# A gated mix of linear attention and a bilinear GLU on one core: thirteen places for h and w_down in the first pair, longer leads for the weights' factors, joint products two steps sooner

## The chip, the cores and the metric

The kernel runs on one NeuronCore of a Trainium2 chip. Its metric is the time of one execution in microseconds (us): the median of three runs before the change is 619.75 us (619.34 to 624.1). All tensors are float32. The matmuls take float32r operands, and every float32 operand is split into a high part (rounded to float32r by a copy) and a low part (the rest), so a product of two operands is three matmuls: high by high, high by low, low by high.

## The reference

The input x has 2048 rows (tokens) of 512. Cut to what matters:

```python
g = sigmoid((x * gate_w).sum(-1, keepdims=True))
# a: linear attention, 32 heads of 16
q, k, v = split_heads(x @ wqkv)
phi = lambda t: where(t > 0, t + 1, exp(t)) + 1e-6
kv  = einsum("bhsd,bhse->bhde", phi(k), v);  z = phi(k).sum over tokens
o   = (phi(q) @ kv) / (phi(q) . z + 1e-6)
a   = o @ wo
# b: bilinear GLU, width F = 1792
h = (x @ w_gate) * (x @ w_up)
b = h @ w_down
return g * a + (1 - g) * b
```

## The kernel before

A first phase computes phi(k) and its products with x for all tokens, and prepares sums of blocks of x. It isn't touched by the change.

The second phase goes over the tokens in two **pairs** of blocks of 512 tokens, and in each pair over 16 **units** (32 in all, numbered n from 0): 14 are of kind "f", one for each 128 columns of F, and two are of kind "q", which make q for half of the heads. A unit multiplies a 2 by 2 arrangement of weight blocks with a 2 by 2 arrangement of blocks of x in seven products of sums of blocks (Strassen's scheme; function `unit`). Each product is six matmuls of 128x512. They go into four PSUM banks Y, X, R and S, each with one buffer, in the order Y X Y R X R S. Between them, by program order, ACT copies Y to m2 (`m` in the profile) and cross, DVE makes R = X - m2, t, S = t - X, and at the end the two products cross that are the two blocks of h. ACT and DVE split these into high and low (tiles `slot`).

All instructions keep the order in which the program writes them, on each engine: ACT, DVE, PE, and the DMA queues of SP and POOL run in order, and an instruction that waits holds all that stand behind it on its engine. So the place of a piece of work in the unit matters. A unit has named **places**, in this order: high, low, e, m, c, d, t, s, r, end. `later(n, place, fn)` puts work at a place, `do` runs it. In a unit ACT also makes the next unit's weights: `w_high` (`wch` in the profile) and the scaled copies for the unit after it (`wr<-wr`), to which POOL adds blocks by DMA (`wr<-in_wgu_add`). SP loads `wr` (`w_load`).

**Down jobs.** Two f units make a group: their two h tiles (high, low) and two w_down tiles are six places. A group gives eight jobs (`down_jobs`), each six matmuls `pdn<-slot,slot` for 128 tokens, scaled and summed into `acc` by DVE. A unit takes jobs from the list at four places, after e, c, t and s, and `shares` tells how many at each: the default is one each, and a table gives other numbers for single units. Jobs not there aren't taken.

**Places for h and w_down.** `slot()` hands out nine tiles of 128x1024 float32r (`SLOTS`) in a circle: three for each f unit, given back when the group's last job has been issued. The w_down tile of a group's first unit is split at "e", that of its second at "r" (`down_weights`), and the split is followed by the next w_down load on SP.

**Mixed units.** In the second pair the four units f4 to f7 (n = 22 to 25) don't make places: their h stays float32 in four tiles `hraw` (scaled by `keep`, two tiles of the pool tag `cb`), since it goes into joint products with the attention's output.

**Output products.** The attention's output is multiplied by a matrix made of kv and wo. This again is a scheme of seven products (`OPROD`), run by `products`. For each product a weight factor is loaded by SP (`w_raw`, `wraw`), has a second block added by POOL (`w_sum`), and is split by ACT and DVE (`w_split`, `owh`, `owl`); the left factor is loaded and added (`load`, `add`, `oraw`) or made from `hraw` (`h_sum`), split at `ready` (`oh`, `ol`), and used by two output jobs of 12 matmuls `po` of 128x256, which `o_down` issues one share later. In the second pair each product has two halves that add up in one bank ("joint"): one of kind "h" with h's blocks and w_down's, and one of kind "o". So there are 28 lines, one a **step**; the second pair has five steps a unit (e, c, t, s, end), the first four (e, c, t, end). Step 0 of the second pair is step 132 counted from unit 0: unit 26, place "t". A weight factor's split stands one step before its first use, its sum two steps before the split, its load four. The factors lie in the tag `cb` (three buffers), the left factors in `z` and `ph` in turn (four each), which before that hold the attention's intermediate tiles (`ex`, `zq`, `zt`, `rb`; `phq`).

After the last unit the last group's eight jobs run, and SP stores the output.

Of the kernel before, what the change touches and what calls it, by code (L numbers as in the profile page):

```python
# [7 lines left out]
F32 = mybir.dt.float32  # L8
F32R = mybir.dt.float32r
# [5 lines left out]
P = 128  # L15
# [8 lines left out]
CH = 512  # L24
# [5 lines left out]
LEAD = 4  # L30
HB = 8
SLOTS = 9
HALF = D // 2


# [27 lines left out]
def gated_mix(ctx: ExitStack, tc, xt, xp, x, wqkv, wq, wq_add, wo, wgu, wgu_add, wdn, gate_w, out):  # L63
# [349 lines left out]
    def unit(n, quad, mixed):  # L413
# [72 lines left out]
        if quad:  # L486
            quad(1, 1, bank["R"])
        elif mixed:
            tt(mixed[:, 1], bank["R"], cross[:, 1], ALU.mult)
        else:  # L490
            hh, hl = hidden()
            tt(cross[:, 1], bank["R"], cross[:, 1], ALU.mult)
            act(hh[:, 1], cross[:, 1])
        do(n, "r")
        product(7, "S")
        if quad:
            quad(0, 0, bank["S"])
        elif mixed:
            tt(mixed[:, 0], bank["S"], cross[:, 0], ALU.mult)
        else:  # L500
            tt(cross[:, 0], bank["S"], cross[:, 0], ALU.mult)

            def high(c):
                act(hh[:, c], cross[:, c])

            def low(c):
                tt(hl[:, c], cross[:, c], hh[:, c].bitcast(F32), ALU.subtract)

            if n + 1 < len(order):

                low(1)
                later(n + 1, "high", lambda: high(0))
                later(n + 1, "low", lambda: low(0))
            else:

                high(0)
                for c in 1, 0:
                    later(n, f"low{c}", lambda c=c: low(c))
            return hh, hl
# [11 lines left out]
    def hidden():  # L531
        return [slot() for _ in "hl"]

    def o_tiles():
        return [p2.tile([P, D], F32R, tag=f"o{v}", name=f"o{v}", bufs=2) for v in "hl"]
# [105 lines left out]
    def down_jobs(pair, group):  # L641
# [3 lines left out]
        def job(i):  # L645
# [12 lines left out]
            for o in range(0, D, step):  # L658
                cols = slice(o, o + step)
                banks.reverse()  # L660
                pd = psum.tile([P, D], F32, tag=banks[0], name="pdn", bufs=2)[:, 0:step]
                for j, ((hh, hl), w2) in enumerate(group):
                    mm3(pd, (hh[:, c, sl], hl[:, c, sl]), [w2[:, v, cols] for v in range(2)], j == 0, j == 1)
                a = acc[pair, i // 2][:, i % 2, cols]
                if first:
                    act(a, pd, scale=s)
                else:
                    stt(a, pd, s, a, ALU.mult, ALU.add)
                if ends:
                    to = nc.gpsimd if pair == 0 else nc.sync  # L670
                    tc.keep_in_program_order(to.dma_start(out[t * P:(t + 1) * P, cols], a))
            todo[0] -= 1
            if not todo[0]:
                for hid, w2 in group:
                    free.extend((*hid, w2))

        return [lambda i=i: job((i + TPP // 2) % TPP) for i in range(TPP)]

# [83 lines left out]
    rows_of_h = {}  # L762

    def products(pair, n0):
        raw, tiles, wt, bank = {}, {}, {}, {}
        steps = STEPS[bool(MIXED[pair])]
        step0 = len(steps) * n0 + 2

        line = [(p, kind, i) for p in range(len(OPROD)) for kind in ("ho" if MIXED[pair] else "o") for i in range(2)]

# [29 lines left out]

        def w_raw(j):
            p, kind, _ = line[2 * j]
            wt[j] = p2.tile([P, 2, HALF], F32, tag="cb", name="wraw", bufs=3)
            dma(wt[j], w_block(p, kind, OPROD[p][1][0]))

        def w_sum(j):
# [56 lines left out]
            later(n, steps[place], lambda: fn(steps[place]))  # L863

        last = len(line)
        for k in range(-5, last):
            if k % 2 and (k + 1) // 2 in range(last // 2):
                at_step(k, lambda place, p=(k + 1) // 2: w_split(p))
            if k >= 0:
                at_step(k, lambda place, k=k: ready(k, place))  # L870
            if 0 <= k + 1 < last:
                at_step(k, lambda place, k=k: h_sum(k + 1))
            if 0 <= k + 3 < last:
                at_step(k, lambda place, k=k: add(k + 3))
            if k % 2 and (k + 3) // 2 in range(last // 2):
                at_step(k, lambda place, p=(k + 3) // 2: w_sum(p))
            if 0 <= k + 5 < last:
                at_step(k, lambda place, k=k: load(k + 5))
            if k % 2 and (k + 5) // 2 in range(last // 2):
                at_step(k, lambda place, p=(k + 5) // 2: w_raw(p))  # L880


    cb = {}
# [64 lines left out]
    for n, (pair, kind, m) in enumerate(order):  # L948
# [3 lines left out]
            banks[0] = "att"  # L952

        def down_weights(n=n, entry=entry):
            entry["d"] = slot()
            split(entry["d"][:, 0], entry["d"][:, 1], wdr.pop(n))
            d_load(ffn.index(n) + 2)

        mixed = None
        if kind == "f" and m in MIXED[pair]:  # L960
            if m == MIXED[pair][0]:
                keep_load(pair)
            mixed = rows_of_h[pair, m] = p2.tile([P, 2, CH], F32, tag="hraw", name="hraw", bufs=4)
# [71 lines left out]
```

## Time and profile before

| | |
|---|---|
| median of three runs | 619.75 us |
| the profiled execution's own time | 621.61 us |
| its span, first to last instruction | 619.6 us |
| TensorE (PE) busy | 599.4 us, 97% |
| weight loads (PEld) | 500.1 us, 81% |
| VectorE (DVE) | 461.7 us, 75% |
| ScalarE (ACT) | 332.9 us, 54% |
| GpSimd (POOL) | 76.8 us, 12% |
| mean granted clock of TensorE | 0.994 |
| bytes moved by DMA | 116.04 MB, mean 187 GB/s |

PE is busy when a matmul is in its pipeline; DMA-issuing instructions are not counted as busy. `SPq` is the queue of SP's sequencer. A row of a timeline gives start, length, engine, line, operation, output<-inputs, count, and in brackets how long the engine was idle before it and whose signal ended that. L71 is the line of every matmul, L77 of every ACT operation, L80 and L83 of the DVE operations, L101 and L104 of the loads and of the adding DMAs, since all are recorded in helpers; so the tiles' names tell what an instruction is. A row of stretches gives each engine's busy time with its count of instructions, then the granted clock, the mean busy share of the 16 DMA engines and GB/s.

The first phase ends at 92.4 us. Then come the units: unit 9 begins at 212 us, unit 16 at 339 us, unit 25 at 460 us, unit 26 at 472 us and unit 31 at 578 us.

### The profile page before, as it was taken

Reading aid. Unit: us, or ns where it says so; the run is one execution under the profiler, and the core shown is the slowest. Engines: PE = TensorE matmul, PEld = TensorE weight load, DVE = VectorE, ACT = ScalarE, POOL = GpSimd, SP = SyncE. Lnnn points to the kernel's source line nnn. Section 1 sums busy time; section 2 is a strip of 40 time slices with the busy share of each in tenths; the row PEclk is TensorE's granted clock in tenths of the full one; section 3 lists DMA queues with packets and bytes.
Section 4 is the critical chain, followed back from the end, with each engine's and each line's share of the span. In section 5 each row is a group of like instructions: output and inputs, shape, how many; then the busy total and the mean of one; then the engine's idle time right before and its main releaser. Section 6 shows DMA issues by size and latency. Waiting matters only on the chain.

```text
span 619.6 us, 8338 instructions
## 1 busy us (share of the span) xinstructions
PE 599.4 (97%) x2898; PEld 500.1 (81%) x2898; DVE 461.7 (75%) x736; ACT 332.9 (54%) x580; POOL 76.8 (12%) x95
## 2 busy tenths in 40 slices
PE   8999999999999989999999899999998789999987
PEld 6888888888888867888888688888877678888876
DVE  6977895755778667777788877666885768778866
ACT  3756756579447644453524658569344556354330
POOL 0011100000011110222011210000101322112000
PEclk9999999999999999999999999999999799999999
DMA  9576949458769868998687867777669987837103
GB/s 295 180 192 146 270 113 291 105 167 209 212 165 267 214 161 231 236 271 215 198 188 191 219 163 176 201 211 224 158 173 270 217 174 191 198 61 187 19 0 135
DMA packets 65803, 116.04 MB, mean 187 GB/s; under 512 B 7969, under 2 KB 29985, under 8 KB 65697
## 3 DMA queue, kind: packets, MB, share of 16 engines
q1 hardware_dynamic: 52816, 77.50, 38.0%
q0 software_dynamic: 12656, 37.49, 34.4%
q10 hardware_dynamic: 288, 0.52, 0.3%
q8 instruction: 22, 0.36, 0.2%
q14 instruction: 21, 0.16, 0.1%
HBM read 97.65 MB, written 19.94 MB: 190 GB/s over the span
## 4 chain that ended last, share of the span: by engine, by line
PE 86%; DVE 5%; DMA 5%; issue 2%; ACT 2%; ACTq 0%; DVEq 0%; POOLq 0%
PE pdn L71 20%; PE bR L71 13%; PE bY L71 13%; PE bX L71 12%; PE po L71 8%; PE pk L71 7%; PE gt L71 7%; PE bS L71 6%; DMA wraw<-wraw 2%; DMA wraw<-in_wdn 1%; DMA wr<-in_wgu 1%; DVE cross L80 1%; DVE ol L80 1%; DMA wraw<-in_wqkv 1%; DVE acc L83 1%
## 5 line engine op out<-in xcount | busy, mean ns | idle before, releaser
L71 PE MATMUL pdn<-slot,slot 128*128 128x512 f32 (+1 forms) x582 | 144.5, 388 | 1.3 <-DVE slot L80 1.3
L71 PEld LDWEIGHTS pdn<-slot,slot 128*128 128x128 f32 x582 | 107.5, 188 | 23.4 <-DVE slot L80 2.1
L83 DVE SCALAR_TENSOR_TENSOR acc<-pdn,gate,acc 128x512 f32<-128x512 f32 (+1 forms) x81 | 59.9, 742 | 23.3 <-PE pdn L71 22.7
L80 DVE TENSOR_TENSOR wcl<-wr,wch 128x512 fp32r<-128x512 f32 (+1 forms) x96 | 73.5, 773 | 3.2 <-ACT wch L77 3.1
L77 ACT ACTIVATE slot<-cross 128x512 fp32r<-128x512 f32 x48 | 30.2, 629 | 77.7 <-DVE cross L80 77.6
L77 ACT ACTIVATE wch<-wr 128x512 fp32r<-128x512 f32 (+1 forms) x96 | 60.4, 694 | 1.6 <-DMA wr<-in_wgu_add 1.5
L71 PE MATMUL po<-owh,oh 128*128 128x256 f32 x168 | 48.4, 288 | 8.9 <-ACT oh L77 8.9
L104 POOL DMA_DIRECT2D wr<-in_wgu_add x28 | 24.2, 865 | 222.3 <-ACT wr L77 137.7
L71 PE MATMUL po<-owh,ol 128*128 128x256 f32 x168 | 48.8, 290 | 3.0 <-DVE ol L80 2.9
L71 PE MATMUL bX<-xbh,wcl 128*128 128x512 f32 x128 | 49.8, 389 | 0.0
L71 PE MATMUL bX<-xbh,wch 128*128 128x512 f32 x128 | 49.8, 389 | 0.0
L71 PE MATMUL bX<-xbl,wch 128*128 128x512 f32 x128 | 49.8, 389 | 0.0
L71 PE MATMUL po<-owl,oh 128*128 128x256 f32 x168 | 48.0, 286 | 0.0
L77 ACT ACTIVATE cross<-bY 128x512 f32<-128x512 f32 x32 | 19.0, 594 | 52.7 <-PE bY L71 52.7
L71 PEld LDWEIGHTS po<-owh,oh 128*128 128x128 f32 x168 | 32.6, 194 | 11.9 <-ACT oh L77 10.3
L80 DVE TENSOR_TENSOR t<-bR,cross 128x512 f32<-128x512 f32 x32 | 22.1, 690 | 23.9 <-PE bR L71 19.6
L77 ACT ACTIVATE wr<-wr 128x512 f32<-128x512 f32 x64 | 36.6, 621 | 4.7 <-DMA wr<-in_wq 2.0
L77 ACT ACTIVATE cross<-bX 128x512 f32<-128x512 f32 x32 | 19.1, 597 | 34.9 <-DVE bS L80 34.8
L71 PEld LDWEIGHTS po<-owh,ol 128*128 128x128 f32 x168 | 32.5, 194 | 4.3 <-DVE ol L80 4.3
L80 DVE TENSOR_TENSOR bR<-bX,m 128x512 f32<-128x512 f32 x32 | 22.3, 697 | 18.0 <-PE bX L71 15.2
L71 PEld LDWEIGHTS po<-owl,oh 128*128 128x128 f32 x168 | 32.6, 194 | 1.2
L80 DVE TENSOR_TENSOR slot<-cross,slot 128x512 fp32r<-128x512 f32 x48 | 32.7, 682 | 0.1
(179 smaller groups left out, 1416.6 us busy)
## 6 DMA issues: line engine op xcount, KB each, us to landing
wr<-in_wgu_add POOLq DMA_DIRECT2D x28, 640.0 KB, 6.9
wr<-in_wgu SPq DMA_DIRECT2D x28, 384.0 KB
wdr<-in_wdn SPq DMA_DIRECT2D x24, 256.0 KB
oraw<-opark POOLq DMA_DIRECT2D x20, 256.0 KB, 6.6
xraw<-in_x SPq DMA_DIRECT2D x16, 256.0 KB
terms<-zq SPq DMA_DIRECT2D x16, 256.0 KB
zt<-terms SPq DMA_DIRECT2D x16, 256.0 KB
rb<-den SPq DMA_DIRECT2D x16, 256.0 KB
```

Of the source, the lines that this page charges most:

```text
L71: tc.keep_in_program_order(nc.tensor.matmul(*args, **kw))
L77: pin(nc.scalar.activation(dst, src, func, **kw))
L80: pin(nc.vector.tensor_tensor(dst, a, b, op=op))
L83: pin(nc.vector.scalar_tensor_tensor(dst, a, scalar, b, op0=op0, op1=op1))
L104: tc.keep_in_program_order(nc.gpsimd.dma_start(dst, src, accum_op=ALU.add))
```

## The change

- The places become thirteen in the first pair: nine as before and four (`EXTRA`) that are tiles of the tag `hraw`, which the mixed units use later. Places are taken by age; in the last four units of the first pair the four extra ones are taken first, and in the second pair only the nine are used.
- In the first pair w_down is split at "e" in both units of a group. In the second pair nothing changes there.
- Shares: unit 4 has (1, 0, 1, 0) instead of (1, 1, 0, 1), so one job less; unit 8 has (1, 0, 1, 0) instead of (0, 1, 0, 1). In the second pair (units 16 to 31) unit 17 takes three jobs instead of two, units 21, 23, 24 and 25 one less each (unit 25 none), and units 26 and 27 two each at "c" and "s" instead of none.
- The joint products of the second pair begin at step 130 instead of 132: unit 26, place "e". They end two steps sooner, so the last two output jobs are issued before the last unit's S instead of after it.
- The weights' factors of the second pair have longer leads: the load stands six steps ahead of the split for factors of kind "h" and five for "o", the sum three for both. In the first pair the leads stay four and two.
- The factors of kind "h" lie in the tags `z` and `ph` in turn instead of `cb`.

No matmul, ACT or DVE operation and no transfer is added or taken away.

```diff
-    shares = {2: (0, 1, 1, 1), 3: (1, 0, 1, 0), 4: (1, 1, 0, 1), 7: (1, 1, 0, 1), 8: (0, 1, 0, 1), 9: (1, 1, 0, 1)}
-    shares.update({units: (1, 2, 1, 2), units + 1: (0, 1, 0, 1)})
-    shares.update({units + m: (0, 1, 0, int(m not in (6, 9))) for m in range(5, 10)})
+    shares = {2: (0, 1, 1, 1), 3: (1, 0, 1, 0), 4: (1, 0, 1, 0), 7: (1, 1, 0, 1), 8: (1, 0, 1, 0), 9: (1, 1, 0, 1)}
+    shares.update({units: (1, 2, 1, 2), units + 1: (1, 1, 1, 0)})
+    shares.update({units + m: (0, 1, 0, 0) for m in range(5, 9)})
+    shares.update({units + 9: (0, 0, 0, 0), units + 10: (0, 1, 0, 1), units + 11: (0, 1, 0, 1)})
...
-    free = [None] * SLOTS
-
-    def slot():
-        some = free.pop(0)
-        if some is None:
-            some = p2.tile([P, 2, CH], F32R, name=f"slot{sum(f is None for f in free)}")
-        return some
+    free = list(range(SLOTS + EXTRA))
+    places = {}
+
+    def slot(n):
+
+        i = min((units - 4 <= n < units and i < SLOTS, age, i) for age, i in enumerate(free) if n < units or i < SLOTS)[-1]
+        free.remove(i)
+        if i not in places:
+            tag = {"tag": "hraw", "bufs": EXTRA} if i >= SLOTS else {}
+            places[i] = p2.tile([P, 2, CH], F32R, name=f"slot{i}", **tag)
+        return i, places[i]
...
-        step0 = len(steps) * n0 + 2
+        step0 = len(steps) * n0 + (0 if MIXED[pair] else 2)
+
+
+        lead = ((6, 3), (5, 3)) if MIXED[pair] else ((4, 2), (4, 2))
...
-            wt[j] = p2.tile([P, 2, HALF], F32, tag="cb", name="wraw", bufs=3)
+            tag = ("z", "ph")[p % 2] if kind == "h" else "cb"
+            wt[j] = p2.tile([P, 2, HALF], F32, tag=tag, name="wraw", bufs=3 if tag == "cb" else 4)
...
-        for k in range(-5, last):
-            if k % 2 and (k + 1) // 2 in range(last // 2):
-                at_step(k, lambda place, p=(k + 1) // 2: w_split(p))
+        def weights(k, ahead, fn):
+
+            for j in range(last // 2):
+                if 2 * j - 1 - (ahead and lead[j % 2][ahead - 1]) == k:
+                    at_step(k, lambda place, j=j: fn(j))
+
+        for k in range(-8, last):
+            weights(k, 0, w_split)
...
-        elif kind == "f" and half:
+        elif kind == "f" and half and pair:
 
             later(n, "r", down_weights)
```

More of the change, by code (lines that the diff above doesn't have):

```diff
@@ L32 @@
 SLOTS = 9
+EXTRA = 4
 HALF = D // 2
@@ L490, in unit @@
         else:
-            hh, hl = hidden()
+            parts_of_h = hidden(n)
+            hh, hl = [part for _, part in parts_of_h]
             tt(cross[:, 1], bank["R"], cross[:, 1], ALU.mult)
@@ L874, in products @@
                 at_step(k, lambda place, k=k: add(k + 3))
[L875 to L876 removed]
+            weights(k, 2, w_sum)
             if 0 <= k + 5 < last:
                 at_step(k, lambda place, k=k: load(k + 5))
[L879 to L880 removed]
+            weights(k, 1, w_raw)
     cb = {}
```

16 lines of the change are left out of this document (8 added, 8 removed).

## The prediction

> **What bounds the kernel now.** I began with the page: TensorE is busy in nearly the whole span.
>
> ```profile
> span 619.6 us, 8338 instructions
> PE 599.4 (97%) x2898; PEld 500.1 (81%) x2898; DVE 461.7 (75%) x736; ACT 332.9 (54%) x580; POOL 76.8 (12%) x95
> ```
>
> So the kernel is bound by TensorE's own list of matmuls, which the change doesn't shorten, and all that can be won is in the 20.2 us in which PE is idle (619.6 - 599.4) and in time at a low clock, if there is any. The next view is the list of PE's waits (total, times, longest, in us).
>
> ```profile
> PE po L71 <- ACT oh L77: 8.9, 4, 5.2
> PE po L71 <- DVE ol L80: 2.9, 4, 1.5
> PE bS L71 <- DVE bS L80: 1.8, 1, 1.8
> PE pdn L71 <- DVE slot L80: 1.3, 2, 0.7
> ```
>
> These are 14.9 us, nearly all of what is idle between start and end, and 11.8 of them stand before po, the matmuls of the joint products. Busy time by stretch (length, then PE, PEld, DVE, ACT, POOL, the granted clock, the DMA share, GB/s) says where.
>
> ```profile
> 222.00:234.00 12.00, 8.91 (x38) 6.50 (x37) 10.04 (x18) 6.71 (x12) 1.72 (x2) 1.00 0.55 101
> 336.00:346.00 10.00, 8.17 (x43) 6.62 (x42) 8.78 (x14) 4.14 (x7) 0.86 (x1) 1.00 0.84 227
> 448.00:460.30 12.30, 12.30 (x56) 10.19 (x55) 10.89 (x19) 4.72 (x8) 0.85 (x1) 1.00 0.62 161
> 460.30:471.70 11.40, 11.14 (x50) 8.90 (x49) 8.96 (x15) 5.87 (x10) 0.85 (x2) 1.00 0.97 268
> 478.00:484.00 6.00, 0.80 (x4) 0.35 (x2) 2.67 (x5) 3.96 (x7) 2.20 (x3) 0.89 1.01 266
> 482.70:489.60 6.90, 5.76 (x19) 4.96 (x20) 4.61 (x8) 3.35 (x7) 1.99 (x3) 0.51 1.09 233
> 490.90:510.50 19.60, 17.50 (x103) 15.07 (x102) 13.51 (x21) 9.26 (x18) 5.30 (x6) 1.00 0.85 179
> ```
>
> The large loss is in units 25 to 27 of 32, where the second pair's joint products begin: 0.26 + 5.20 + 2.10 us idle, and 5.76 busy us at a clock of 0.51, of which 0.49 x 5.76 = 2.8 are lost. Together **10.4 us**. Two smaller ones lie in the first pair (3.1 and 1.8 us); a third is shown below.
>
> **The change, part by part.** Units of work, from the chain of waits: seven products a unit, a down job and an output job of a product cost
>
> ```profile
> 92.56 1.36 PE bY L71 x6
> 117.92 1.36 PE pdn L71 x6
> 271.52 1.43 PE po L71 x12
> ```
>
> so a bare unit is 9.5 us. No matmul is added or removed; down jobs change places.
>
> (A) *Start of the joint products.* In time order, the stall came about so (start, length, engine, what, and in brackets the idle time before it):
>
> ```profile
> 466.30 0.48 SPq L101 DMA_DIRECT2D wraw<-in_wdn  x1
> 471.70 1.22 POOL L104 DMA_DIRECT2D wraw<-in_wdn  x1 [1.06 <-DMA wraw<-in_wdn]
> 479.82 0.63 ACT L77 ACTIVATE owh<-wraw 128x512 fp32r<-128x512 f32 x1 [3.27 <-DMA wraw<-in_wdn]
> 480.36 1.86 ACT L77 ACTIVATE wch<-wr 128x512 fp32r<-128x512 f32 x3
> 482.13 1.13 ACT L77 ACTIVATE wr<-wr 128x512 f32<-128x512 f32 x2
> 483.17 0.61 ACT L77 ACTIVATE oh<-oraw 128x512 fp32r<-128x512 f32 x1
> 483.84 0.58 PE L71 MATMUL po<-owh,oh 128*128 128x256 f32 x1 [5.20 <-ACT oh L77]
> ```
>
> The first weight factor is loaded at 466.30, its second block is added from 471.70 and is there 8.1 us later; ACT, in order, then does the split, three wch and two wr before the oh that PE wants. After the change the load is issued four steps of program order sooner (two for the lead of 6, two for the earlier start), the add stands at "c" of unit 25 and the split at its "end"; oh comes at "e" of unit 26, before the wch and wr. Unit 26 also gets a down job ahead of the first product, 1.36 us of cover that wasn't there. I work out what is left. The factor's place is now one of z, so SP must wait for the opark store that reads that place:
>
> ```profile
> 458.29 3.11 SPq L101 DMA_DIRECT2D opark<-rb  x2
> 462.15 0.63 SPq L101 DMA_DIRECT2D wr<-in_wgu  x1
> 468.35 1.15 ACT L77 ACTIVATE wr<-wr 128x512 f32<-128x512 f32 x2 [0.89 <-DMA wr<-in_wgu]
> 473.20 1.37 PE bX L71 x6
> ```
>
> That wait isn't in this trace. From below: den is issued at 450.64 and the rb that needs it landed goes out at 452.74, 2.1 us. From above: a cbs load issued at 215.64 ended ACT's wait at 222.67, 7.0 us.
>
> ```profile
> 450.64 1.17 SPq L101 DMA_DIRECT2D den<-den  x2
> 452.74 2.56 SPq L101 DMA_DIRECT2D rb<-den  x4
> 215.64 0.46 SPq L101 DMA_DIRECT2D cbs<-in_xp  x1
> 222.67 0.63 ACT L77 ACTIVATE cbs<-cbs 128x512 f32<-128x512 f32 x1 [4.79 <-DMA wr<-in_wgu]
> ```
>
> With the DMA share at 0.97 there I take 6.6, near the upper end: SP stands from 458.3 to 464.9, and behind it stand two opark stores, a phq store and the load of unit 27's wr. With issues of 0.38 to 0.63 us the wr load leaves at about 466.5 instead of 462.15; its old flight to ACT was 6.2 us, with a shorter queue ahead I take 4, so ACT's two wr start at 470.5 and end at 471.6, and cross<-bX, 0.6 like the other ACT rows, at 472.2. Units 24 and 25 each lost a down job, so PE wants bank X for unit 26 at 473.2 - 2.7 = 470.5: **1.7 us** stall. The factor's load lands at about 469.5 and its add after 5 to 8 us (8.1 above, alone on the queue I take 5); ACT does owh (0.63) and m (0.60) and PE, ready for its second Y at 472.2 + 1.4 = 473.6, gets it at 475.7: **2.1 us**. The first product's third matmul needs ol, which on DVE stands behind owl, oraw, bR, two keep and a w_down half, six of 0.7: about **1 us**. In unit 27 I expect none, since later factors have two or three steps of 3.4 us. Left: 4.8 us. Bounds: 1 us if the store lands after 2.1; 10.4 as now if all waits add up. I take the nearer to the rows worked here, 4.8: gain 10.4 - 4.8 = **5.6 us**.
>
> The Trainium skill, "TensorE: Matmul & The Clock Gate", section "What's actually happening", says that the clock drops to half after one idle window of about 3.4 us and that the window runs free. The trace agrees: 5.2 us idle brought 0.51, pauses of 1.8 us left 1.00. By that rule two pauses of 1.7 and 2.1 us keep the clock unless they merge; merged, it would be 2.8 us less gained and about 612 us.
>
> (B) *First pair.* In seven units (1, 4, 6, 9, 11, 13, 15) the split of w_down moves from "r", at the end, to "e". At 341 us one sees what it did at "r":
>
> ```profile
> 341.09 0.61 ACT L77 ACTIVATE slot<-wdr 128x512 fp32r<-128x512 f32 x1
> 341.73 0.69 DVE L80 TENSOR_TENSOR slot<-wdr,slot 128x512 fp32r<-128x512 f32 x1 [1.22 <-ACT slot L77]
> 344.28 0.38 PE L71 MATMUL po<-owh,ol 128*128 128x256 f32 x1 [1.51 <-DVE ol L80]
> 300.32 0.39 PE L71 MATMUL po<-owh,ol 128*128 128x256 f32 x1 [0.87 <-DVE ol L80]
> 231.72 0.50 PE L71 MATMUL pdn<-slot,slot 128*128 128x512 f32 x1 [0.62 <-DVE slot L80]
> ```
>
> DVE waits 1.22 us for ACT, spends 0.69, and everything behind it, ol included, is 1.9 us later; PE loses 1.8 us in that stretch (10.00 - 8.17), 1.51 of it for ol. Without it ol is there in time: 1.8 us here, and by the same chain 0.9 at 300. At 231 the first down job of unit 10 needs h and w_down of unit 9, just made. With one down job less in unit 4, each group of eight is now eaten one job late, so this first job is of the older group: 1.3 us (the two waits of pdn for slot). That is what the places are for: six of the group being read, up to six of the next, thirteen in all, so nothing waits for a place. Sum **4.0 us**. At "e" the same 0.61 and 0.69 us stand behind m and before cross<-bY; PE has X, a down job and Y to do there, 4 us, which hides them; without that cover 0.7 us a unit, 4.9 in all, is the lower bound of this part (-0.9), 4.0 the upper. The next w_down load is issued earlier on SP; it finds its buffer free. The 1.8 us before bS come from the cbs load above and stay.
>
> (C) *The end.* The two last output jobs leave the tail:
>
> ```profile
> 601.21 0.68 DVE L80 TENSOR_TENSOR cross<-bS,cross 128x512 f32<-128x512 f32 x1
> 603.13 0.39 PE L71 MATMUL po<-owh,oh 128*128 128x256 f32 x1 [1.69 <-ACT oh L77]
> 605.14 11.14 PE L71 MATMUL pdn<-slot,slot 128*128 128x512 f32 x54
> ```
>
> PE is idle from 601.4 (603.13 - 1.69), after one output job of 1.43, so the last S ended at 600.0, and pdn begins at 605.14: 5.1 us with 2.9 of work, 2.3 lost. After, DVE does cross (to 601.9), then the low part of h, 0.7 (602.6), for which the last matmul of the first down job waits; without it that matmul would start at 600.0 + 5/6 x 1.36 = 601.1. So 1.5 lost, gain **0.8 us** (0 to 2.3).
>
> Thinner units 21 to 25 (four jobs fewer, given to 26 and 27) cost nothing as long as the weights come; unit 25, the thinnest of them now with one down job, is the stretch from 460.3 with 0.26 us idle. If they don't, up to 4 x 1.36 = 5.4 us.
>
> Sum: 5.6 + 4.0 + 0.8 = **10.4 us**. The profiled execution took 621.6 us (span 619.6 and 2.0 around it), so 611.2 for it; the median of the three runs is 1.9 us lower, 619.75, and becomes **609.3 us**. A change under 1% (6.2 us) is about what this kernel's measurement can't tell from none.
>
> **The rivals.**
>
> *The DMA engines set the pace at the joint start.* From 460.3 to 491 the share is 0.97 to 1.09; the same bytes must pass before PE can go on, so longer leads only queue them longer. For it: those rows. Against: from 448 to 460.3 it is 0.62 and the old loads were sent late. Then PE gets through unit 26 no sooner, and of (A) only the 2.1 us in unit 27 come: 619.75 - 2.1 - 4.8 = 613. The Trainium skill, "DMA: Bandwidth & Descriptors", section "Issuing engines are not separate DMA queues", speaks for this one: transfers of all issuers share the same 16 engines and interleave, and by it a lead helps only while these have room. The shares quoted agree.
>
> *All of it is hidden.* The store lands in some 2 to 3 us and the wr load keeps its place: 1 us is left in (A), gain 9.4: 605.5.
>
> *The w_down split only moves its wait.* If DVE at "e" is as late as at "r", (B) is -0.9 to 0: 613 to 614.
>
> *Slower: SP's stand before z.* Each us that the opark store lands later holds unit 27's wr load, ACT's wr, cross<-bX and bank X by one. At 6.6 us it costs 1.7. Once PE is idle 4 us at a stretch the clock halves as it did, 2.8 us more. A stand of s costs s - 6.6 + 2.8 more than the forecast, so from s = 14.2 us on all 10.4 us are gone; at 17 us the kernel takes 622.5, at 21 us 626.5. Against it: no landing in these rows is above 8.1 us.
>
> **How the numbers follow.** Forecast 609.3 (606 to 612.5): 0.50. Hidden, 605.5: 0.13. DMA pace, 613: 0.18, half of it under 613.5. (B) void, 613.5: 0.11, half (0.05) under it. Slower: 0.08, of it 0.05 so long that it is over 1%. Faster by over 1% is below 613.5: 0.50 + 0.13 + 0.09 + 0.05 = 0.77; slower 0.05; same the rest, 0.18. The range, 603.5 to 615.5, takes in the bounds of (A) and (B), and leaves out the slow rival and the far ends.
>
> **What would show it.** (A): PE's wait for oh at 5.2 gone, the clock 1.00 throughout, small waits of bX or bY on ACT at the start of unit 26, owh's wait for the add before m. (B): PE's waits for ol at the starts of units 14 and 16 and for slot in unit 10 gone, the wait before S in unit 9 kept. (C): one wait of 1 to 2 us of pdn after the last S. I am wrong if SP stands longer than 7 us at the first factor, if the clock dips again, or if new waits of cross<-bY or wch on the add appear in units 21 to 25.

## The result and the profile after

The changed kernel takes 616.24 us (median of 20 runs, 614.96 to 620.62) against 621.44 us for the kernel before (20 runs, 618.45 to 624.1). The ratio is 0.9928, 95% interval 0.991 to 0.9945: 0.7% faster (4.5 us by the ratio, 5.2 by the medians), where 10.4 us were forecast; 1.7 us of the distance to the forecast time is in its base, the 619.75 us of three runs. The page of the profiled execution and PE's waits (total, times, longest, in us), in two fences; source lines from L72 on are one higher than before:

```profile
span 613.8 us, 8334 instructions
PE 598.3 (97%) x2898; PEld 499.2 (81%) x2898; DVE 461.9 (75%) x736; ACT 332.7 (54%) x580; POOL 76.2 (12%) x95
PEclk9999999999999999999999999999998999999999
```

```profile
PE bX L72 <- ACT cross L78: 4.0, 1, 4.0
PE bY L72 <- ACT m L78: 3.4, 3, 1.8
PE po L72 <- DVE acc L81: 1.7, 1, 1.7
...
PE pdn L72 <- DVE slot L81: 0.9, 2, 0.7
PE po L72 <- DVE ol L81: 0.8, 2, 0.6
```

The 8.9 us for oh are gone, as are the 1.8 of bS and most of those for ol (2.9 to 0.8); the waits for slot in unit 10 (1.3) are gone too, and the 0.9 listed now stand at the end. In their place come 4.0 us for bank X, 3.4 for m and 1.7 for acc, of which the kernel before has only 0.3, for m. The slice with an 8 in PEclk shows that the clock fell again.

Stretches of before and after tell where. The rows are units 9, 10 and 16, and then units 25 to 27 (before in one row, after one by one with the time at half clock between); the columns are those of the prediction.

```profile
211.65:227.31 15.66, 13.89 (x62) 11.19 (x61) 8.82 (x14) 6.00 (x11) 1.72 (x2) 1.00 0.75 189
227.31:244.16 16.85, 15.53 (x68) 12.31 (x66) 14.53 (x24) 6.79 (x12) 0.86 (x1) 1.00 0.75 192
...
339.06:360.88 21.82, 19.99 (x91) 15.90 (x90) 19.16 (x27) 11.94 (x18) 5.28 (x8) 1.00 0.91 216
460.25:510.53 50.28, 42.72 (x205) 35.44 (x204) 33.64 (x53) 23.44 (x42) 12.42 (x13) 0.93 0.94 220
```

```profile
210.91:224.86 13.95, 13.89 (x61) 11.18 (x60) 9.63 (x16) 6.79 (x12) 1.70 (x2) 1.00 0.81 223
224.86:239.84 14.98, 14.98 (x67) 12.39 (x66) 13.83 (x23) 6.39 (x11) 0.85 (x1) 1.00 0.75 178
333.63:353.51 19.88, 19.70 (x91) 15.97 (x90) 18.43 (x26) 11.43 (x17) 4.34 (x7) 1.00 0.87 218
451.11:462.07 10.96, 9.81 (x43) 7.81 (x42) 8.77 (x14) 4.23 (x7) 0.00 (x0) 1.00 0.72 178
462.07:487.03 24.96, 18.62 (x91) 15.01 (x90) 13.66 (x22) 11.03 (x20) 10.06 (x11) 0.93 1.06 266
467.70:471.12 3.42, 2.68 (x6) 1.57 (x6) 1.13 (x2) 0.14 (x1) 1.50 (x3) 0.50 1.09 299
487.03:508.59 21.56, 19.91 (x115) 17.42 (x114) 16.91 (x27) 10.25 (x19) 4.43 (x5) 1.00 0.82 182
```

Units 9, 10 and 16 lost their gaps: 1.7, 1.9 and 1.9 us shorter with the same matmuls; with 1.1 in unit 14 (21.92 to 20.80) that is 6.6 us. Units 25 to 27 grew from 50.3 to 57.5 us. Three down jobs more (4 x 1.36 come, 1.36 goes) and two output jobs (2 x 1.43) are 6.9 us of that, so the loss in them is what it was: 11.8 us before, 12.0 after. The whole account of the spans, work that moved between units taken out:

| stretch | change in us |
|---|---|
| before unit 4 (nothing changed there) | +0.6 |
| units 9, 10, 14, 16 | -6.6 |
| units 22 and 23 | +1.0 |
| units 25 to 27 | +0.25 |
| units 28 to 30 | -0.4 |
| unit 31 and the end (42.04 to 38.52, 2.86 of work moved out) | -0.7 |
| sum (619.6 to 613.8) | -5.8 |

So the whole gain is the first pair's, and the joint products' start gave nothing. In time order, the timeline of after there (start, length, engine, what, in brackets the idle time before it):

```profile
450.69 0.38 SPq L102 DMA_DIRECT2D opark<-rb  x1
...
455.14 0.50 PE L72 MATMUL bY<-xc4h,wch 128*128 128x512 f32 x1 [1.15 <-ACT m L78]
...
458.71 0.38 SPq L102 DMA_DIRECT2D wraw<-in_wdn  x1
...
460.22 0.48 SPq L102 DMA_DIRECT2D wr<-in_wgu  x1
...
463.12 1.20 POOL L105 DMA_DIRECT2D wraw<-in_wdn  x1 [13.07 <-DMA wraw<-in_wdn]
...
465.87 1.15 ACT L78 ACTIVATE wr<-wr 128x512 f32<-128x512 f32 x2 [6.16 <-DMA wr<-in_wgu]
466.93 0.58 ACT L78 ACTIVATE cross<-bX 128x512 f32<-128x512 f32 x1
...
467.56 0.69 PE L72 MATMUL bX<-xbh,wch 128*128 128x512 f32 x1 [3.97 <-ACT cross L78]
...
470.98 0.63 ACT L78 ACTIVATE owh<-wraw 128x512 fp32r<-128x512 f32 x1 [3.47 <-DMA wraw<-in_wdn]
471.51 0.58 ACT L78 ACTIVATE m<-bY 128x512 f32<-128x512 f32 x1
...
472.14 0.51 PE L72 MATMUL bY<-xc4h,wch 128*128 128x512 f32 x1 [1.76 <-ACT m L78]
```

SP issues the store that reads the z place at 450.69 and nothing more until 458.71: it stands 8.0 us until that store is there. In the list of SP's waits from 450 to 460 us this is the row

```profile
SPq L102 <- DMA opark<-rb: 7.6, 1, 7.6
```

The DMA packets in the trace show what fills this time: until 454.0 SP's queue still moves transfers issued earlier, the store's own 256 packets begin at 455.3 and the last at 458.3, and GpSimd's add to the next weights (wr<-in_wgu_add, issued 449.20, landed 458.26) runs between and beside them. Behind the stand the load of unit 27's wr goes out at 460.22 and lands as ACT starts at 465.87, 5.65 us later; cross<-bX follows in order, and PE, idle since 463.59, gets bank X at 467.56. Then ACT waits for the factor's add (issued 463.12, there by 470.98, 7.9 us later) with m behind it, and PE waits again. The first wait was long enough to halve the clock from 467.70 to 471.12.

### The profile page after: what moved, and what is told of

It reads as the page before. It is cut to its first block, busy times and chain, and to the rows that moved or that the text cites. A ratio compares the mean times of both kernels' runs of the same rounds, so it can differ in the third digit from the quotient of the medians.

```text
span 613.8 us, 8334 instructions
## 1 busy us (share of the span) xinstructions
PE 598.3 (97%) x2898; PEld 499.2 (81%) x2898; DVE 461.9 (75%) x736; ACT 332.7 (54%) x580; POOL 76.2 (12%) x95
## 5 line engine op out<-in xcount | busy, mean ns | idle before, releaser
L72 PE MATMUL pdn<-slot,slot 128*128 128x512 f32 (+1 forms) x582 | 144.9, 388 | 0.9 <-DVE slot L81 0.9
L72 PEld LDWEIGHTS pdn<-slot,slot 128*128 128x128 f32 x582 | 107.4, 188 | 23.2 <-DVE slot L81 1.6
L72 PE MATMUL bX<-xbh,wch 128*128 128x512 f32 x128 | 50.3, 393 | 4.0 <-ACT cross L78 4.0
L72 PE MATMUL bX<-xbh,wcl 128*128 128x512 f32 x128 | 50.3, 393 | 0.0
L72 PE MATMUL bX<-xbl,wch 128*128 128x512 f32 x128 | 50.3, 393 | 0.0
L72 PE MATMUL po<-owh,oh 128*128 128x256 f32 x168 | 47.4, 282 | 1.7 <-DVE acc L81 1.7
L72 PE MATMUL po<-owh,ol 128*128 128x256 f32 x168 | 47.8, 285 | 0.8 <-DVE ol L81 0.8
L72 PE MATMUL po<-owl,oh 128*128 128x256 f32 x168 | 47.5, 283 | 0.0
L78 ACT ACTIVATE wr<-wr 128x512 f32<-128x512 f32 x64 | 36.6, 623 | 12.7 <-DMA wr<-in_wgu 9.4
L81 DVE TENSOR_TENSOR bR<-bX,m 128x512 f32<-128x512 f32 x32 | 22.3, 697 | 19.0 <-PE bX L72 16.2
L72 PEld LDWEIGHTS po<-owh,oh 128*128 128x128 f32 x168 | 32.1, 191 | 3.3 <-DVE acc L81 1.9
L72 PEld LDWEIGHTS po<-owl,oh 128*128 128x128 f32 x168 | 32.1, 191 | 1.4
L72 PEld LDWEIGHTS po<-owh,ol 128*128 128x128 f32 x168 | 32.1, 191 | 1.3 <-DVE ol L81 1.2
```

The costliest lines, as they stand in the source:

```text
L72: tc.keep_in_program_order(nc.tensor.matmul(*args, **kw))
L78: pin(nc.scalar.activation(dst, src, func, **kw))
L81: pin(nc.vector.tensor_tensor(dst, a, b, op=op))
```

## The experiments

Each is compared by its ratio to the kernel before, run with it on the same chip; times in us are medians.

| run | us | ratio, 95% interval |
|---|---|---|
| the change | 616.24 | 0.9928 (0.991 to 0.9945) |
| e1, second pair's part alone | 624.37 | 1.0058 (1.0036 to 1.0081) |
| e2, first pair's part alone | 613.09 | 0.9881 (0.9857 to 0.9905) |
| e3, first factor in ph | 613.45 | 0.9874 (0.985 to 0.9899) |
| e4, jobs stay in units 21 to 25 | 614.02 | 0.9904 (0.987 to 0.9939) |
| e5, first pair, split at r | 618.73 | 0.9959 (0.9938 to 0.998) |
| e6, first pair, unit 4 keeps its job | 615.42 | 0.9905 (0.9878 to 0.9931) |
| e7, e3 with the split a step later | 612.61 | 0.9863 (0.9838 to 0.9889) |
| e8, first factor from unit 23 | 611.85 | 0.985 (0.9823 to 0.9878) |
| e9, first add left out | 614.66 | 0.9891 (0.9871 to 0.9911) |
| e10, e3 and e4 together | 609.73 | 0.9817 (0.9794 to 0.984) |
| e11, e8 and e4 together | 608.62 | 0.9803 (0.978 to 0.9825) |
| e12, e11 with the o factor a step sooner | 608.26 | 0.9805 (0.9779 to 0.9832) |

### The two parts apart: e1 and e2

e1 keeps the change's second pair and has the first pair as before:

```diff
-    shares = {2: (0, 1, 1, 1), 3: (1, 0, 1, 0), 4: (1, 0, 1, 0), 7: (1, 1, 0, 1), 8: (1, 0, 1, 0), 9: (1, 1, 0, 1)}
+    shares = {2: (0, 1, 1, 1), 3: (1, 0, 1, 0), 4: (1, 1, 0, 1), 7: (1, 1, 0, 1), 8: (0, 1, 0, 1), 9: (1, 1, 0, 1)}
...
-    free = list(range(SLOTS + EXTRA))
+    free = list(range(SLOTS))
...
-        i = min((units - 4 <= n < units and i < SLOTS, age, i) for age, i in enumerate(free) if n < units or i < SLOTS)[-1]
+        i = free[0]
...
-        elif kind == "f" and half and pair:
+        elif kind == "f" and half:
```

> The second pair is that of the change (joint products two steps sooner, longer leads, first factors in z and ph, its shares), the first pair is that of before. Theory, the stand of SP: in the changed kernel units 25 to 27 lost 1.4 + 8.4 + 2.2 = 12.0 us against their bare work, before they lost 11.8, so this part alone gains nothing there and only the end's 0.7 us: within 1 us of before, the wait of bX for ACT (4.0 us) is there. Rival, that all parts help alike: 2.5 us or more below before.

e2 keeps the change's first pair and has the second as before, with unit 17 at three jobs:

```diff
-    shares.update({units + m: (0, 1, 0, 0) for m in range(5, 9)})
-    shares.update({units + 9: (0, 0, 0, 0), units + 10: (0, 1, 0, 1), units + 11: (0, 1, 0, 1)})
+    shares.update({units + m: (0, 1, 0, int(m not in (6, 9))) for m in range(5, 10)})
...
-        step0 = len(steps) * n0 + (0 if MIXED[pair] else 2)
+        step0 = len(steps) * n0 + 2
...
-        lead = ((6, 3), (5, 3)) if MIXED[pair] else ((4, 2), (4, 2))
+        lead = ((4, 2), (4, 2))
...
-            tag = ("z", "ph")[p % 2] if kind == "h" else "cb"
+            tag = "cb"
```

> The first pair is that of the change (thirteen places, w_down split at e, shares of units 4 and 8), the second that of before, with unit 17 at three jobs. Theory: units 9, 10, 14 and 16 gain 1.7 + 1.9 + 1.1 + 1.9 = 6.6 us by the two traces, so the median is 5 to 6.5 us below before, as good as the whole change or better. Rival, that all parts help alike: about 2.5 us below before. The wait of po for oh of 5.2 us is still there.

Measured: the second pair's part alone makes the kernel 0.58% slower, the first pair's alone 1.19% faster. The product of the two ratios, 0.9938, lies in the interval of the change's 0.9928, so within the noise the two parts just add. Neither of e1's expectations came (within 1 us of before, or 2.5 us below it): it is 2.8 us above by the medians. Its PE waits 3.9 us for X, as the change does, but its stretch at half clock is three times as long and costs half of 7.08 busy us, 3.5, where the change loses 1.3 (and that execution was the fastest of its nine):

```profile
472.34:482.57 10.23, 7.08 (x16) 5.10 (x17) 5.95 (x10) 4.98 (x9) 4.71 (x5) 0.50 1.07 262
```

And e2 still has the large wait of the kernel before, and is nevertheless faster than the whole change. It gained more than its 5 to 6.5 us, 7.4 by the ratio and 8.5 by the medians; in its trace units 9, 10, 14 and 16 give 7.0, and units 26 and 27, whose program is that of before, 1.1 more (37.7 us for 38.9); why is open. From its list of PE's waits:

```profile
PE po L72 <- ACT oh L78: 8.3, 2, 6.6
```

### What in the first pair gains: e5 and e6

e5 is e2 with the split of w_down at "r" again in every group's second unit, seven units of the first pair; its expectation names units 4 and 8, which was too few.

```diff
-        elif kind == "f" and half and pair:
+        elif kind == "f" and half:

             later(n, "r", down_weights)
```

> The first pair's change with its thirteen places and its moved jobs, the second pair as before (as in the run of the first pair alone, 613.1 us), but w_down of units 4 and 8 split at step "r" of the unit behind, where the kernel before has it, instead of at "e" of its own unit. Theory 'places': what is gained comes from the free places and the later split of the joint slots' jobs, and the step of the w_down split is indifferent: 613 us, within 1 us, units 9 and 10 at 13.6 and 15.0 us as with "e". Theory 'split': the earlier split takes VectorE's 0.9 us pieces out of units 5 and 9 and so is what shortened unit 9 by 1.7 us; then unit 9 is back at 15 us or more and the time is 614.5 to 615.5 us.

e6 is e2 with the jobs of units 4 and 17 as before, so that no job is pushed behind:

```diff
-    shares = {2: (0, 1, 1, 1), 3: (1, 0, 1, 0), 4: (1, 0, 1, 0), 7: (1, 1, 0, 1), 8: (1, 0, 1, 0), 9: (1, 1, 0, 1)}
-    shares.update({units: (1, 2, 1, 2), units + 1: (1, 1, 1, 0)})
+    shares = {2: (0, 1, 1, 1), 3: (1, 0, 1, 0), 4: (1, 1, 0, 1), 7: (1, 1, 0, 1), 8: (1, 0, 1, 0), 9: (1, 1, 0, 1)}
+    shares.update({units: (1, 2, 1, 2), units + 1: (0, 1, 0, 1)})
```

> The first pair's change, the second pair as before, but unit 4 takes three jobs again and unit 17 two, so that no down-projection job is pushed behind: the places are thirteen in number, the backlog of jobs is that of the kernel before. Theory 'places': the places alone free units 9 to 16 of their waits for a slot, so the time stays at 613 us, with unit 4 back at 13.6 us and unit 17 at 12.3 us. Theory 'backlog': the jobs moved from unit 4 to unit 17 are what gives units 10 to 16 their slack; without them the waits in units 10 and 14 come back and the time is 615 to 617 us.

In e5 the waits for ol are back, with the same DVE row as before the change (1.22 us for ACT's half of the split), and units 14 and 16 are 21.93 and 21.60 us long again, 1.1 and 1.7 more than in e2 (20.80 and 19.88). PE's waits, and a row of the timeline:

```profile
PE po L72 <- DVE ol L81: 3.0, 4, 1.5
```

```profile
336.55 0.69 DVE L81 TENSOR_TENSOR slot<-wdr,slot 128x512 fp32r<-128x512 f32 x1 [1.22 <-ACT slot L78]
```

Unit 10 stayed at 14.96 us. In e6 it is the other way round: unit 14 stays at 20.80, unit 10 waits (16.25 us long, 15.26 busy):

```profile
225.33:241.58 16.25, 15.26 (x68) 12.32 (x66) 13.93 (x23) 6.27 (x11) 0.86 (x1) 1.00 0.74 185
```

So the earlier split is what units 14 and 16 gain (1.1 of 1.1 and 1.7 of 1.9 us), and the job moved from unit 4 to unit 17 is 1.3 of the 1.9 us of unit 10; the other 0.6 stay gained without it. Both theories that made the detail matter were right, though not in all they named: e5 is 4.8 us (0.78%) slower than e2 where 1.5 to 2.5 were expected, and not in unit 9; in e6 the wait in unit 14 did not come back, and its time, inside the 615 to 617 us expected, can't be told from e2's by the intervals, so the reading rests on unit 10 of its trace. Of e5's 4.8 us its trace shows only 3.0, but the profiled execution was the fastest of its runs. Unit 9 is 15.66 and 14.96 us long in the two traces with the old first pair and 13.60 to 14.74 in the twelve with the new one, e5 (14.40) and e6 (14.06) among them. So neither the split nor the moved job is needed for it; what e5 and e6 share with the rest, the thirteen places and unit 8's shares, was not tried alone. The twelve differ by 1.1 us among themselves, so some of the 1.7 us may be scatter.

### What the joint start loses: e3, e4, e7, e8 and e9

e3 only swaps the order of the tags, so that the first factor takes a place of ph, which is free sooner:

```diff
-            tag = ("z", "ph")[p % 2] if kind == "h" else "cb"
+            tag = ("ph", "z")[p % 2] if kind == "h" else "cb"
```

> The changed kernel with z and ph exchanged for the factors of kind h, so that the first one takes a place whose last reader is a DVE operation that SP has waited for anyway; nothing else moves. Theory, the stand of SP: the load of unit 27's weights leaves 3 to 5 us sooner, the wait of bX for ACT (4.0 us) goes, the clock stays whole, and the kernel is 3 to 5 us below the change (about 612). Rival, the DMA engines set the pace: the loads leave sooner and land no sooner, and the time stays within 1.5 us of the change (about 616).

SP and ACT in the timeline of e3:

```profile
451.22 0.38 SPq L102 DMA_DIRECT2D opark<-rb  x1
451.64 1.06 SPq L102 DMA_DIRECT2D wraw<-in_wdn  x1
...
454.83 0.99 SPq L102 DMA_DIRECT2D wr<-in_wgu  x1
...
468.85 0.63 ACT L78 ACTIVATE owh<-wraw 128x512 fp32r<-128x512 f32 x1 [4.39 <-DMA wraw<-in_wdn]
469.39 0.58 ACT L78 ACTIVATE m<-bY 128x512 f32<-128x512 f32 x1
```

The stand is gone, and so is the wait for X, since wr leaves 5.4 us sooner; the time is 0.54% (3.4 us) under the change's. The clock did not stay whole as expected: it is halved from 471.34 to 474.75. The reason is m, which behind owh now costs 3.6 us in one wait: owh starts 5.3 us into unit 26 (which begins at 463.5) instead of 8.9, and PE, no longer held for X, is there sooner still.

e9 leaves that add out (the first joint product then uses one weight block where the reference's needs the sum of two) and keeps the stand:

```diff
-            for block in OPROD[p][1][1:]:
+            for block in OPROD[p][1][1:] if j or not MIXED[pair] else ():
                 dma_add(wt[j], w_block(p, kind, block))
```

> The whole change as it is, but the first joint product's w factor of h is used without the second block that GpSimd's transfer adds to it (one transfer of 512 KB left out, so the result is of other weights). Theory 'SyncE's stand': SyncE still stands before the z place in unit 25, the load of w_gate_up's next block still goes out behind it, and TensorE's wait for bank X in unit 26 stays near 4.0 us; only the wait for m behind the factor's copy (1.8 us) goes, and the time is 613.5 to 614.5 us. Theory 'the add's landing': ScalarE and the queues are held by the 7.8 us of that add; without it both waits in unit 26 shrink below 1 us and the time is 610 to 611.5 us, about that of the run with the early factor (611.85 us).

```profile
450.13 0.38 SPq L102 DMA_DIRECT2D opark<-rb  x1
457.99 0.39 SPq L102 DMA_DIRECT2D wraw<-in_wdn  x1
```

```profile
PE bX L72 <- ACT cross L78: 3.0, 1, 3.0
```

SP stands 7.9 us without the factor's add, bank X is waited for 3.0 us, and the clock is halved from 467.40 to 470.81. The time, 614.66, is next to what the theory of SP's stand gave (613.5 to 614.5) and 3 us off the other's. So the stand makes the wait for X, not the factor's add, whose absence takes 1.0 us from it. GpSimd's add to wr is still in flight during the stand here (issued 448.56, landed 457.58), as in the change; no run leaves that one out, so how much of the stand is its doing was not tried.

e7 is e3 with the split of that factor one step later, behind m (the copy of bank Y; the expectation's words "softmax numerators" don't fit it):

```diff
-                if 2 * j - 1 - (ahead and lead[j % 2][ahead - 1]) == k:
+                if 2 * j - 1 - (ahead and lead[j % 2][ahead - 1]) + (not j and not ahead and bool(MIXED[pair])) == k:
```

> The whole change with the first w factor of h in a ph place and the second in a z place (as in the run at 613.45 us), and ScalarE's and VectorE's split of that first factor one step later, at "e" of unit 26, behind the softmax numerators m of that step. Theory 'order on ScalarE': m waited 3.6 us in unit 26 only because ScalarE's copy of the factor, itself waiting for the transfer, stood ahead of it; with the copy behind m that wait falls below 1 us and the time to 610.5 to 611.5 us. Theory 'the loss only moves': the copy is then late for the first joint product, which waits some 3 us in its place, and the time stays within 1 us of 613.4 us.

```profile
PE po L72 <- ACT oh L78: 2.1, 1, 2.1
...
PE bY L72 <- ACT m L78: 1.5, 2, 1.0
```

The 3.6 us for m are gone and 2.1 us for oh stand in their place: the loss moves, as the rival said, and the time is within 1 us of e3's. The order on ACT was not the cause; the add is there too late for either.

e8 therefore starts the first factor earlier, in the third buffer of cb, loaded at "c" and added to at the end of unit 23:

```diff
-            tag = ("ph", "z")[p % 2] if kind == "h" else "cb"
+            tag = ("cb", "ph")[j] if MIXED[pair] and j < 2 else ("ph", "z")[p % 2] if kind == "h" else "cb"
...
-                if 2 * j - 1 - (ahead and lead[j % 2][ahead - 1]) == k:
+                if 2 * j - 1 - (ahead and ((13, 10) if MIXED[pair] and not j else lead[j % 2])[ahead - 1]) == k:
...
-        for k in range(-8, last):
+        for k in range(-14, last):
```

> The whole change, but the first w factor of h is read into the third buffer of cb, which is free by then, at step "c" of unit 23 and added to at the end of unit 23, seven steps sooner; the second is in a ph place, the others as in the run at 613.45 us. SyncE stands before no z place in unit 25. Theory 'the add's landing': 7.7 us from issue to landing of the second half's add, behind the broadcasts of r, is what holds ScalarE; taken out of units 25 and 26, both the wait for cross and the 3.6 us for m in unit 26 go, and the time is 609 to 610.5 us. Theory 'the transfers are merely many': the six joint factors load the DMA engines as before and another of them is late, so that units 26 and 27 together stay at 42 us and the time at 613 us.

```profile
PE bY L72 <- ACT m L78: 2.0, 2, 1.5
PE po L72 <- DVE acc L81: 1.7, 1, 1.7
PE po L72 <- DVE ol L81: 1.3, 4, 0.6
```

Both waits of unit 26 that the change had, for X and for m, are gone, and in the profiled execution the clock stays at 1.00 to the end (four of its six runs have a mean of 0.994 to 0.997, so there it fell); 611.85 us lies between the two theories, and the intervals of e8 and e3 overlap. Units 26 and 27 still take 41.6 us, since the next supplies (ol, the o factor, acc) are late by smaller sums.

What is left of m, 1.5 us, stands in unit 25. e4 asks for the price of the thin units: it is the change with the second pair's jobs left where they were.

```diff
-    shares.update({units + m: (0, 1, 0, 0) for m in range(5, 9)})
-    shares.update({units + 9: (0, 0, 0, 0), units + 10: (0, 1, 0, 1), units + 11: (0, 1, 0, 1)})
+    shares.update({units + m: (0, 1, 0, int(m not in (6, 9))) for m in range(5, 10)})
```

> The changed kernel with the second pair's shares as before (unit 17 at three): units 21, 23, 24 and 25 keep their down jobs and units 26 and 27 have none. Theory, the stand of SP: the stores of opark and the weights get 5.4 us more before unit 26, which shortens the wait of bX by about as much, but 26 and 27 have 5.4 us less to cover the factors with: within 2 us of the change. Rival, the thin units are what costs: the 1.15 us in unit 25 and the 4.0 us of bX go and the kernel is 3 us or more below the change.

Alone it gives 0.24%, and the intervals of e4 and the change overlap; the rival's 3 us or more did not come. In the trace the 0.5 us in unit 22 and 0.9 of the 1.15 in unit 25 are gone, and the wait for X is 0.7 instead of 4.0, since PE comes to it later; 2.9 us for m in unit 26 are there instead.

### Together: e10, e11 and e12

e10 has e3's and e4's edits, e11 e8's and e4's, and e12 besides loads and adds the first o factor one step sooner:

```diff
-                if 2 * j - 1 - (ahead and ((13, 10) if MIXED[pair] and not j else lead[j % 2])[ahead - 1]) == k:
+                if 2 * j - 1 - (ahead and (((13, 10), (6, 4))[j] if MIXED[pair] and j < 2 else lead[j % 2])[ahead - 1]) == k:
```

> Two small edits together: the first w factor of h in a ph place (alone 613.45 us) and the second pair's jobs left in units 21 to 25 (alone 614.0 us), each 2.2 to 2.8 us under the change's 616.2 us. Theory 'two causes': SyncE's stand and the thin units lose time in different places, the gains add for the most part, 611 to 612 us. Theory 'one cause': both only give the same late transfers more time, and together they reach no more than the better one, 613 to 614 us.

> The first w factor of h from unit 23 (alone 611.85 us) with the second pair's jobs left in units 21 to 25. Theory 'thin units': the 0.5 us wait in unit 22, the late reciprocals of unit 25 (1.5 us) and part of the waits in unit 26 come from units too short for ScalarE and the broadcasts; with the jobs back they go, 609.5 to 610.5 us. Theory 'supplies at the joint start': the first o factor's add, 7.2 us from issue to landing, and the blocks of h are what units 26 and 27 wait for; with the jobs back in front they start no sooner against them and the time stays at 611 to 612.5 us.

> As the run before it, and the first o factor also loaded and added to one step sooner (leads 6 and 4 for 5 and 3). Theory: ScalarE waits 5.0 us for that factor's add in unit 26 and TensorE 1.1 us behind it; a step sooner (some 4 us) takes that 1.1 us away, 0.5 to 1 us below the run without it. Rival: its load then stands in front of the stores of unit 25's numerators on SyncE and delays the blocks of opark that the first o products read; the time is the same or up to 1 us longer.

e10 gains 1.11% on the change, clearly more than e3's 0.54 alone: two causes, as its first theory said, and its time is even below that theory's 611 to 612 us. That it is also more than 0.54 and 0.24 together lies within the noise; a reason for it would be the clock, which doesn't fall in e10 and does in e3 and e4. e11 is under its range too (608.62 for 609.5 to 610.5), and 0.47% under e8, so the jobs are worth more in the thin units than behind them; e10 and e11 can't be told apart by their intervals. In e12 PE's wait for oh falls from 1.1 to 0.4 us, but the ratio doesn't tell it from e11. e12's units 25, 26 and 27, and PE's largest waits:

```profile
453.10:464.64 11.54, 11.18 (x50) 8.94 (x48) 9.10 (x15) 6.39 (x11) 0.86 (x1) 1.00 1.03 312
464.64:481.60 16.96, 14.66 (x80) 12.38 (x78) 12.49 (x21) 8.88 (x16) 7.79 (x9) 1.00 1.08 252
481.60:499.97 18.37, 17.28 (x103) 15.18 (x102) 14.51 (x24) 9.92 (x18) 3.96 (x5) 1.00 0.90 205
```

```profile
PE po L72 <- DVE ol L81: 2.1, 3, 1.7
...
PE po L72 <- ACT oh L78: 0.4, 1, 0.4
PE bY L72 <- ACT m L78: 0.4, 1, 0.4
```

The DMA engines are as full in unit 26 as in the change (1.08 and 1.06), at a clock of 1.00 and with 2.3 us of PE idle instead of 6.3. They are full in unit 25 too, where the change's stand left them at 0.72. e12 is 2.0% faster than the kernel before (ratio 0.9805), 1.2% more than the change.

## Why the prediction was wrong, step by step

**(A), the start of the joint products: 5.6 us forecast, about -1 found.** This is the part that failed. The mechanism was named, SP's stand before the z place, then wr, ACT's wr, cross, bank X, and after it m behind owh. Its first two terms were too small, and three were put at nothing: the clock, unit 27 and the thin units.

- SP's stand: 6.6 us taken, 8.0 measured, outside the bounds of 2.1 and 7.0. Both bounds came from rows of other transfers at other times, and the 6.6 lay inside them by choice. The row behind the 7.0 names the load of wr, issued at 216.20, and not that of cbs. The store itself could be seen in the trace of before: its 256 packets are through some 6.7 us after its issue there (458.29 to about 465.0), 7.6 us in the change.
- wr's flight: 4 us taken "with a shorter queue ahead", 5.65 measured. The two errors are 3.05 us. PE was ready for X 12.9 us after the store's issue (463.59), where 12.2 were forecast (470.5 after 458.3), so 0.7 of that was covered, and the wait for X is 3.97 for 1.7.
- m in unit 26 (2.1 forecast, 1.76 found) came out near by luck: from the store's issue on, the add is there after 20.3 us where 16.2 were forecast (its own time is 7.9 us for 5), and PE wants its second Y after 19.7 for 15.3, so two errors cancel. ol (1 and 0.61) is near too, but the forecast gives no sum for it: six operations of 0.7 are 4.2 us, and how 1 us is left of them isn't worked out.
- The clock: "two pauses of 1.7 and 2.1 us keep the clock" failed with the first term, at 3.97. The period at 0.50 costs half of its 2.68 busy us, 1.3; nothing was set down for it.
- "In unit 27 I expect none": 1.65 us for acc, an operation that stands on DVE in a row of others without a pause (it starts at 493.13); the forecast looked at the factors alone. The thinner units "cost nothing as long as the weights come": 0.5 in unit 22, 0.2 in 23, 1.15 in 25, where m stands on ACT behind two phq, which wait 2.85 and 0.57 us for rb of DVE. e4 and e11 show that most of this goes when the jobs stay.

Together 3.97 + 1.76 + 0.61 + 1.3 + 1.65 + 1.85 = 11.1 us where 4.8 were forecast, against 10.4 in the kernel before. Of the prediction's signs of error, the stand longer than 7 us and the dip of the clock came. New waits in units 21 to 25 came too, but PE's are for m behind phq and not for what was named; ACT's wait for the add before wch is 0.4 us in unit 25.

**(B), the first pair: 4.0 forecast, 6.6 found.** By its terms: in unit 16 1.8 forecast and 1.9 found, in unit 14 0.9 and 1.1, each with the cause that e5 shows; in unit 10 1.3 and 1.9, of which e6 gives the moved job just the 1.3. The split at "e" was hidden as said: units 6, 11, 13 and 15 kept their length. Not foreseen was unit 9, 1.7 us in this trace: "The 1.8 us before bS come from the cbs load above and stay" was wrong. That load leaves 2.5 us after the unit's start instead of 4.0, behind stores of terms that land sooner. Why they do is open.

**(C), the end: 0.8 forecast, 0.66 found**, with one wait of 0.7 us for slot after the last S, where 1 to 2 were named.

**The rivals.** The time, 616.24, lies above all the faster rivals (613 to 614 the nearest) and below the slower one. "The DMA engines set the pace" gave 613 and is only half refuted. The engines are full in unit 26 in both kernels, but e12 gets through units 26 and 27, which have four down jobs less there, in 35.3 us, with 3.4 us idle against the change's 8.0 in 46.5. It has less left to move there: by the rows' GB/s unit 25 of e12 moves 3.6 MB and unit 26 4.3, in the change 1.95 and 6.6, since SP stood through most of unit 25. The Trainium skill, "DMA: Bandwidth & Descriptors", section "Issuing engines are not separate DMA queues", says that transfers of all issuers interleave on the same 16 engines; the 8.0 us of the store and 7.9 of the add, beside shares of 0.72 to 1.09, agree. By the packets above the store's 8.0 us go mostly in what is already in flight on the engines, though no run tried that alone; the order in which SP and ACT stand decides who waits for it and how much is left for the full stretch, and e3, e8 and e9 show that the change lost by the order. The slower rival had the right mechanism, at 8.0 us of stand where it needed 14: e1 is that rival without the first pair's gain, 0.58% slower. And the sum hid that (B) and (A) erred to opposite sides; the error of (A) alone, 6.6 us, is larger than that of the whole (10.4 forecast, 5.8 found in the spans).

## What to carry to other kernels

When a load gets a buffer that a store must leave first, the price is the store's full landing time in that stretch (7.5 to 8.0 us in the change, e1, e4 and e9), and the queue's next loads pay it too; look for a buffer whose reader is done earlier before counting on a longer lead. Work moved out of units ahead of a stall takes away the time in which supplies arrive; here it was better left there (e10 and e11). Bounds for a landing time should come from the same queue at the same fill of the engines, and a landing taken from elsewhere needs a bound above the longest one seen, not below.

## What the runs showed of the hardware

The half clock comes in steps: the stretches at 0.50 inside the runs last 3.41, 6.83 or 10.24 us, one, two or three times 3.413, and in e7 two of them begin 20.48 us apart, six times that. The Trainium skill, "TensorE: Matmul & The Clock Gate", section "What's actually happening", gives a free-running window of 3413 ns, and these numbers agree. It also says that the clock drops after an idle window. Here the window didn't have to be idle throughout. Two windows of e7 and one of e10, each of 3.41 us, the first two followed by their 3.42 us at half clock:

```profile
467.36:470.77 3.41, 1.09 (x5) 0.46 (x3) 1.74 (x4) 2.10 (x4) 0.98 (x2) 1.00 1.08 241
470.77:474.19 3.42, 3.42 (x13) 3.15 (x14) 0.46 (x1) 0.05 (x1) 1.07 (x1) 0.50 1.08 254
487.84:491.25 3.41, 1.75 (x12) 1.33 (x12) 3.41 (x7) 1.62 (x3) 0.00 (x0) 1.00 1.08 286
491.25:494.67 3.42, 3.42 (x11) 2.75 (x10) 0.49 (x1) 0.38 (x1) 0.90 (x1) 0.50 0.94 305
```

```profile
467.64:471.05 3.41, 1.59 (x8) 0.97 (x6) 0.00 (x0) 0.46 (x1) 1.68 (x2) 1.00 1.11 294
```

In e7 PE was busy 1.09 and 1.75 us of the two windows, and both times the clock fell; in e10 it was busy 1.59 us, and the clock stayed. Over all fourteen traces, from 100 us to PE's last matmul and with windows counted back from where the clock fell: the nine entered at full clock with PE idle for 57% or more were all followed by half clock, of ten between 48 and 54% two were, and none below. In that band the share alone doesn't decide: 49% idle halved the clock in e7, 53% didn't in e10. So here a pause of 1.66 us (e7) can halve the clock if it falls inside one window, and one of 2.9 us (e4) needn't if two windows share it. The prediction's limit of 4 us at a stretch was too generous.

GpSimd's adding transfers are slow per byte here: in the traces of before, after and e12 its packets of 5120 bytes take 404 ns each by the median, 12.7 bytes a ns, and SP's packets of 4096 bytes 159 ns, 25.8 bytes a ns.
